# Two linear and two windowed attention layers, forward and backward: score halves at the end of a pass, sums tile by tile, one ring of PSUM banks

## The chip, the cores and the metric

The kernel runs on one core of a Trainium2 chip. The metric is the device time of one execution in microseconds (us); less is better. The engines are TensorE (PE; PEld is its weight loads), VectorE (DVE), ScalarE (ACT), GpSimd (POOL) and SyncE (SP), which issues most DMAs. Matmul results land in PSUM, eight banks of 512 float32 columns for each of 128 partitions; PE writes them, DVE and ACT read them.

## The reference

Four layers over x of 2048 x 640 (bfloat16), 32 heads of 20 columns, then the gradients of the input and of the four weights. A is linear attention, B is softmax attention over the last 256 positions. A and B are applied twice with the same weights.

```python
def _A_ref(x, wqkv, wo):
    ...
    phi = lambda t: jnp.where(t > 0, t + 1, jnp.exp(t)) + 1e-6
    pq, pk = phi(q), phi(k)
    kv = jnp.einsum("bhsd,bhse->bhde", pk, v)
    z = jnp.einsum("bhsd->bhd", pk)
    num = jnp.einsum("bhqd,bhde->bhqe", pq, kv)
    den = jnp.einsum("bhqd,bhd->bhq", pq, z)[..., None] + 1e-6
    o = num / den
    ...
def _B_ref(x, wqkv, wo):
    ...
    scores = jnp.einsum("bhqd,bhkd->bhqk", q, k) * (Dh ** -0.5)
    mask = (idx[:, None] - idx[None, :] >= 0) & (idx[:, None] - idx[None, :] < W)
    scores = jnp.where(mask[None, None], scores, -1e9)
    p = _softmax(scores, axis=-1)
    o = jnp.einsum("bhqk,bhkd->bhqd", p, v)
    ...
x = x + _A_ref(_layernorm(x, axis=-1), A_wqkv, A_wo)
x = x + _B_ref(_layernorm(x, axis=-1), B_wqkv, B_wo)
x = x + _A_ref(_layernorm(x, axis=-1), A_wqkv, A_wo)
x = x + _B_ref(_layernorm(x, axis=-1), B_wqkv, B_wo)
```

kv and z of an A layer are sums over all 2048 positions: no position of the layer's output can be had before the last position has been added.

## The kernel before

Positions are cut into 16 tiles of 128 (tt, or b in the B layers), and columns into five blocks of 128 (m). The forward function has a first part for layer 0, which computes keys and values of all tiles (`a_first`, `a_qkv`), and two passes, `ab_pass(0)` and `ab_pass(2)`. A pass takes each tile through the rest of an A layer (`a_num`: products with the sums; `out_proj` with Wo_A) and the following B layer (`b_qkv`, `attn`, `out_proj` with Wo_B). The first pass also runs `a_first` of layer 2, some two tiles behind; the second pass also prepares gradients of the output (`dO`, with its multiplication on POOL at L830).

The order of the work is made by a planner (`Sched`). Each piece of work names its engine, an estimated duration, and the things that it reads and writes; pieces are listed by a due time in tiles. The planner then runs a list schedule over the engines: the earliest ready piece comes first, and on PE a piece may overtake at most twelve others. What results is a fixed order for each engine. On the chip each engine works through its order and waits where data isn't there.

The sums. In layer 0 `kv_tile` (L609, L611) adds one tile at a time to two PSUM banks, as soon as keys and values of the tile are there. For layer 2 `a_kv` does it after all tiles, one column block at a time over 16 tiles (L571), and z after them (L583), in the banks of the general ring. The sums are multiplied by a block mask into `mbd` (L590), z is copied (L595) and spread over the heads (L597); `a_num` uses both at L647 and L480, and DVE's first use of its result is `rt` (L651).

B attention. A tile has eight groups (g) of four heads. `scores` computes a group's scores for three key tiles (nkt is 3 from the third tile on) in twelve matmuls of 128 columns (L734); head hh uses rows 32 hh to 32 hh + 31 of PE's array and bank hh of the four-bank tile `s_ps`. ACT takes the exponential of all four banks at once into an `e_sb` buffer, of which there are three (L739). POOL masks the diagonal in two instructions of two heads each (L743) and the far edge of the second two heads (L751), DVE that of the first two (L748). `values` multiplies with v (L768), two heads at a time (p_ is 0 or 1), into `pv_ps`, one bank for sixteen heads; DVE reads it at L775 and L776.

The eight PSUM banks of the passes are three of the general ring `mm_ps` (projections, transposes, a_num), four of `s_ps` and one of `pv_ps`. In a ring with `free=True` a piece takes whichever bank is free first, and the last free bank is kept for the piece that is next in the list.

`dO_start` clears two slabs on DVE (L792) in memory that held keys and values of tiles 13 and 14.

Of the kernel before, what the change touches and what calls it, by code (L numbers as in the profile page):

```python
# [11 lines left out]
ALU = mybir.AluOpType  # L12
# [4 lines left out]
P = 128  # L17
# [212 lines left out]
class Kern:  # L230
# [130 lines left out]
    def forward(self):  # L361
# [7 lines left out]
        with ExitStack() as st:  # L369
# [194 lines left out]
            def a_kv(l):  # L564
                def band_sum(m, lo, hi):
                    w_ = hi - lo
                    ps = R["mm"].buf()
                    for t0 in range(0, TT, 4):
                        def f(t0=t0):
                            for tt in range(t0, t0 + 4):  # L570
                                nc.tensor.matmul(ps.t[:, 0:w_], lhsT=pk(tt, m * P, (m + 1) * P), rhs=vv(tt, lo, hi),  # L571
                                                 start=(tt == 0), stop=(tt == TT - 1))
                        op("PE", pe([w_] * 4), f, [k for tt in range(t0, t0 + 4) for k in
                                                   (("pk", tt, 2), ("pk", tt, 3), ("vv", tt, 4), ("vv", tt, 5))], [ps])
                    masked(m, ps, 0)

                for m in range(DT):
                    band_sum(m, *self.band[m])
                zp = R["mm"].buf()
                for m in range(DT):  # L580
                    def f(m=m):
                        for tt in range(TT):
                            nc.tensor.matmul(zp.t[:, m:m + 1], lhsT=pk(tt, m * P, (m + 1) * P),  # L583
                                             rhs=self.ones_bf[:, 0:1], start=(tt == 0), stop=(tt == TT - 1))
                    op("PE", pe([1] * TT), f, [("pk", tt, i) for tt in range(TT) for i in (2, 3)], [zp])
                store_mbd(l, zp, 0)

            def masked(m, ps, off):
                lo, hi = self.band[m]
                op("DVE", vp(hi - lo), lambda: nc.vector.tensor_mul(  # L590
                    mbd[:, m, lo:hi], ps.t[:, off:off + hi - lo], self.bmask[:, m, 0:hi - lo]), [ps, "masks", "zeros"],
                   [("mbd", m)])

            def store_mbd(l, zp, off):
                op("DVE", vp(DT), lambda: nc.vector.tensor_copy(zcol, zp.t[:, off:off + DT]), [zp], ["zcol"])  # L595
# [7 lines left out]
            def kv_tile(tt, sums):  # L603

                def f():
                    for m, (lo, hi) in enumerate(self.band):
                        i, off = at_[m]
                        lhsT = pk(tt, m * P, (m + 1) * P)
                        nc.tensor.matmul(sums[i].t[:, off:off + hi - lo], lhsT=lhsT, rhs=vv(tt, lo, hi),  # L609
                                         start=(tt == 0 and m == 0), stop=(tt == TT - 1), skip_group_check=True)  # L610
                        nc.tensor.matmul(sums[1].t[:, zoff + m:zoff + m + 1], lhsT=lhsT, rhs=self.ones_bf[:, 0:1],  # L611
                                         start=(tt == 0 and m == 0), stop=(tt == TT - 1), skip_group_check=True)
                op("PE", pe([hi - lo for lo, hi in self.band] + [1] * DT), f,
                   [("pk", tt, 2), ("pk", tt, 3), ("vv", tt, 4), ("vv", tt, 5)], sums)
# [100 lines left out]
            def attn(l, b, qT, kTs, vts, oT, out):  # L715
# [10 lines left out]
                def scores(g):  # L726
                    def f():
                        s = R["s"].buf()

                        def mm_s():  # L730
                            for j in range(nkt):
                                for hh in range(4):
                                    r = slice(HPAD * hh, HPAD * (hh + 1))
                                    nc.tensor.matmul(s.t[:, hh, j * P:(j + 1) * P], lhsT=kTs[j].t[r, g, :],  # L734
                                                     rhs=qT.t[r, g, :], start=True, stop=True,
                                                     tile_position=(HPAD * hh, 0))
                        op("PE", 210 + 55 * nkt, mm_s, [qT] + kTs, [s])
                        e = es[g] = R["e"].buf()
                        op("ACT", av(4 * nkt * P), lambda: nc.scalar.activation(  # L739
                            e.t[:, :, 0:nkt, :], s.t[:, :, 0:nkt * P].rearrange("p h (i q) -> p h i q", q=P),  # L740
                            ACT.Exp, scale=self.c_att), [s], [(e, p_, j) for p_ in (0, 1) for j in range(nkt)])
# [14 lines left out]
                def values(g, p_):  # L756
                    def f():
                        e = es[g]
                        q = 4 * g // 16
                        if q not in pvs:  # L760
                            pvs[q] = R["pv"].buf()
                        pv = pvs[q]

                        def mm_pv():
                            for hh in (2 * p_, 2 * p_ + 1):
                                h = 4 * g + hh
                                for j in range(nkt):
                                    nc.tensor.matmul(pv.t[:, h % 16, :], lhsT=e.t[:, hh, j, :],  # L768
# [3 lines left out]
                        if g % 4 == 3 and p_ == 1:  # L772
                            h0 = 16 * q
                            li = lambda: lv.t[:, i_, h0:h0 + 16]
                            op("DVE", 200, lambda: nc.vector.reciprocal(li(), pv.t[:, :, DH]), [pv], [(lv, i_, q)])  # L775
                            op("DVE", vp(16 * DH), lambda: nc.vector.tensor_tensor(  # L776
                                out=o.t[:, h0 * DH:(h0 + 16) * DH].rearrange("p (h d) -> p h d", d=DH),
                                in0=pv.t[:, :, 0:DH], in1=li().unsqueeze(2).to_broadcast([P, 16, DH]), op=ALU.mult),
# [146 lines left out]
            def ab_pass(l, last):  # L925
# [81 lines left out]
                else:  # L1007
                    a_first(items, l + 2, 2.09, -0.2)
                run(items)
# [779 lines left out]
```

## Time and profile before

| | us |
|---|---|
| median of 3 runs (lowest, highest) | 2114.66 (2114.49, 2114.9) |
| profiled execution | 2109.33 |
| its span, first to last instruction | 2107.4 |
| layer 0's keys, values and sums | up to about 77 |
| first pass, last exponential's end | 387.26 |
| first use of layer 2's sums on DVE | 409.11 |
| second pass, last exponential's end | 700.59 |
| first scores of the backward phase on PE | 706.27 |

A line of the timeline gives start, duration, engine, line of the program, operation, what it writes and reads, and how many instructions were merged; in brackets the idle time before it and who ended it. A row of the windows gives, for a stretch, each engine's busy time and number of instructions, the clock that PE was granted, the DMA engines' share and their rate. A row of the waits gives who waited for whom, and the sum, the number of times and the longest. Matmuls are pipelined: the duration of one is its latency, and what it costs is the distance from start to start.

### The profile page before, as it was taken

To read this page: it belongs to the slowest core of one execution; us is meant where nothing else is said; L and a number is where in the kernel's file an instruction comes from. 1 tells how busy PE (TensorE), PEld (TensorE's weight loads), DVE (VectorE), ACT (ScalarE), POOL (GpSimd) and SP (SyncE) were. 2 spreads that over 40 slices of the span, in tenths; PEclk is the share of its full clock that TensorE was granted. 3 is DMA by queue.
4 is the path that set the end of the run, shared out by engine and by line. 5 is a ranking of instruction groups with operands and counts; after the bars stand their busy time and mean duration, and the time that the engine had idled before them with its cause. 6 is when DMAs were issued, how large, how long until landed. Compare 5 with 4: busy or idle time off the path is not lost. (4 is left out here: it accounts for less than half of the span.)

```text
span 2107.4 us, 68065 instructions
## 1 busy us (share of the span) xinstructions
PE 1982.7 (94%) x28001; PEld 1362.9 (65%) x28001; DVE 1437.3 (68%) x2978; ACT 1169.3 (55%) x1946; POOL 840.8 (40%) x1851
## 2 busy tenths in 40 slices
PE   7889999799898899999999999999999999999999
PEld 5656555566555577777665677656777776666764
DVE  8767776567776799999143369606999994444641
ACT  5367888358777688887222223215888872211330
POOL 1044555236666666665022213203666652221210
PEclk9999999899999899999999999998999999999999
DMA  8689877379998699997999999738889879899973
GB/s 309 196 189 216 180 180 184 109 175 195 211 202 191 129 151 165 159 156 122 190 200 191 256 209 207 181 97 159 139 144 144 147 122 183 190 204 241 212 172 90
DMA packets 926568, 373.72 MB, mean 177 GB/s; under 512 B 816944, under 2 KB 902960, under 8 KB 926000
## 3 DMA queue, kind: packets, MB, share of 16 engines
q1 hardware_dynamic: 885616, 337.77, 79.3%
q10 hardware_dynamic: 40640, 31.60, 5.2%
q8 instruction: 219, 3.59, 0.7%
q14 instruction: 93, 0.76, 0.1%
HBM read 106.73 MB, written 112.23 MB: 104 GB/s over the span
## 5 line engine op out<-in xcount | busy, mean ns | idle before, releaser
L1606 DVE SCALAR_TENSOR_TENSOR ds_sb<-pair,e_sb 128x768 bf16<-128x768 f32 x480 | 439.4, 952 | 18.8 <-POOL e_sb L1595 6.8
L1591 ACT ACTIVATE e_sb<-pair 128x768 bf16<-128x768 f32 x480 | 379.1, 812 | 96.1 <-PE pair L1571 94.8
L739 ACT ACTIVATE e_sb<-s_ps 128x1536 bf16<-128x1536 f32 (+2 forms) x256 | 350.6, 1370 | 98.7 <-PE s_ps L734 56.6
L743 POOL TENSOR_SCALAR_AFFINE_SELECT e_sb<-e_sb 128x256 bf16<-128x256 bf16 x512 | 213.2, 439 | 378.2 <-ACT e_sb L739 361.0
L1098 PEld LDWEIGHTS <-om 128*128 128x128 bf16 x1920 | 188.3, 98 | 157.0 <-DMA om<-o 2.2
L1098 PE MATMUL mm_ps<-wq,dqT 128*128 128x320 bf16 x1920 | 276.0, 299 | 4.7 <-ACT dqkv L1430 3.7
L1259 POOL TENSOR_TENSOR gw<-w,gcar 128x640 f32<-128x640 f32 x64 | 89.9, 1405 | 456.7 <-ACT w L1256 451.2
L1098 PE MATMUL mm_ps<-dqkv,om 128*128 128x480 bf16 x1280 | 268.9, 367 | 1.4 <-DMA om<-hn 1.4
L1598 POOL TENSOR_SCALAR_AFFINE_SELECT e_sb<-e_sb 128x256 bf16<-128x256 bf16 x448 | 182.1, 406 | 199.9 <-ACT e_sb L1591 199.9
L1595 POOL TENSOR_SCALAR_AFFINE_SELECT e_sb<-e_sb 128x256 bf16<-128x256 bf16 x512 | 206.5, 407 | 78.5 <-ACT e_sb L1591 78.5
L1098 PEld LDWEIGHTS <-dqT 128*128 128x128 bf16 x1920 | 185.9, 98 | 79.0 <-issue 6.6
L1241 ACT ACTIVATE dh<-mm_ps 128x320 f32<-128x320 f32 x128 | 56.0, 437 | 292.0 <-PE mm_ps L1098 234.3
L1624 PE MATMUL dsT_ps<-ident,ds_sb 128*128 128x128 bf16 x2244 | 189.5, 221 | 3.8 <-DVE dsT L1627 1.3
L480 PE MATMUL mm_ps<-Wqkv_B,hnTB 128*128 128x320 bf16 x960 | 180.4, 300 | 10.7 <-DMA hnTB<-hnB 6.5
L768 PEld LDWEIGHTS <-e_sb 128*128 128x128 bf16 x2880 | 122.2, 97 | 74.7 <-POOL e_sb L751 20.0
L768 PE MATMUL pv_ps<-v_slab,e_sb 128*128 128x32 bf16 x2880 | 145.0, 178 | 19.0 <-DVE oB L776 4.6
L1627 DVE COPY dsT<-dsT_ps 128x768 bf16<-128x768 bf16 x268 | 147.8, 552 | 7.7 <-PE dsT_ps L1624 4.7
L480 PE MATMUL mm_ps<-Wqkv_A,pqT 128*128 128x320 bf16 x780 | 139.2, 302 | 5.8 <-DVE oA L657 2.4
L1571 PE MATMUL pair<-VTg,dOTg 32*128 32x384 bf16 (+2 forms) x896 | 139.9, 318 | 1.0 <-ACT e_sb L1591 0.3
L1624 PEld LDWEIGHTS <-ds_sb 128*128 128x128 bf16 x2244 | 132.4, 98 | 12.1 <-issue 9.3
L1645 PE MATMUL dqvk_ps<-Qsl,ds_sb 128*128 128x32 bf16 x2880 | 134.7, 177 | 3.2 <-ACT dqkv L1627 2.7
L1261 DVE SCALAR_TENSOR_TENSOR gcar<-hn,sm,gw 128x640 bf16<-128x640 bf16 x64 | 80.4, 1256 | 82.0 <-POOL gw L1259 82.0
(178 smaller groups left out, 3556.5 us busy)
## 6 DMA issues: line engine op xcount, KB each, us to landing
qkvp<-qk_slab SPq DMA_DIRECT2D x32, 512.0 KB, 3.1
om<-o SPq DMA_DIRECT2D x20, 512.0 KB, 5.9
hn<-hn SPq DMA_DIRECT2D x64, 160.0 KB, 3.0
om<-hn SPq DMA_DIRECT2D x20, 512.0 KB, 4.9
ee<-e SPq DMA_DIRECT2D x32, 320.0 KB, 3.7
e<-ee SPq DMA_DIRECT2D x52, 160.0 KB, 2.0
qkvp<-v_slab SPq DMA_DIRECT2D x32, 256.0 KB, 2.7
o<-o SPq DMA_DIRECT2D x48, 160.0 KB, 3.4
```

The lines of the kernel that those rows point to most:

```text
L480: nc.tensor.matmul(ps.t[:, w0:w0 + width], lhsT=lhsT(), rhs=rhs(), start=start, stop=stop)
L739: op("ACT", av(4 * nkt * P), lambda: nc.scalar.activation(e.t[:, :, 0:nkt, :], s.t[:, :, 0:nkt * P].rearrange("p h (i q) -> p h i q", q=P) ...
L743: op("POOL", 440, lambda p_=p_: nc.gpsimd.affine_select(out=e.t[:, 2 * p_:2 * p_ + 2, nkt - 1, :], in_=e.t[:, 2 * p_:2 * p_ + 2, nkt - 1, ...
L768: nc.tensor.matmul(pv.t[:, h % 16, :], lhsT=e.t[:, hh, j, :], rhs=vts[j].t[:, h, :], start=(j == 0), stop=(j == nkt - 1))
L1098: nc.tensor.matmul(ps.t[:, w0:w0 + width], lhsT=lhsT(), rhs=rhs(), start=start, stop=stop)
L1571: nc.tensor.matmul(ps[:, i, c0:c0 + len(ks) * P], lhsT=ld[g][lhs][r, q * P:(q + 1) * P], rhs=ld[g][rhs][r, ks[0] * P:(ks[-1] + 1) * P], st ...
L1591: nc.scalar.activation(e, PR[h][:, :, 0:3 * P].rearrange("p i (j q) -> p i j q", q=P), ACT.Exp, scale=self.c_att)
L1595: nc.gpsimd.affine_select(out=e[:, :, j, :], in_=e[:, :, j, :], compare_op=ALU.is_ge, fill=0.0, base=0, pattern=[[0, 2], [-1, P]], channel ...
L1598: nc.gpsimd.affine_select(out=e[:, :, j, :], in_=e[:, :, j, :], compare_op=ALU.is_ge, fill=0.0, base=-1, pattern=[[0, 2], [1, P]], channel ...
L1606: nc.vector.scalar_tensor_tensor(out=DS[n][:, hs], in0=PR[h][:, :, 0:3 * P].rearrange("p i (j q) -> p i j q", q=P), scalar=self.c_att, in1 ...
L1624: nc.tensor.transpose(ps[:, i, j, :], DS[n][:, 2 * p + i, j, :], self.ident)
L1627: (nc.vector.tensor_copy if eng == "DVE" else nc.scalar.copy)(out, in_)
```

## The change

- In the last twelve groups of a pass (b is 14 with g from 4, and b is 15) scores and exponential are made in two halves of two heads, each with its own two banks of `s_ps` as its key. All other groups are as before. Masks and values are unchanged, but a mask now depends on its own half.
- `a_kv` is gone. `kv_tile` is used for layer 2 too, listed in the first pass behind its scores; the sums lie in banks 2 and 3 of `s_ps`, so the first tile waits for the last second-half exponential, and the second pass's scores wait until `store_mbd` has read the sums. All five masked products and z's copy follow the last tile.
- `pv_ps` is gone; `values` takes a bank of `mm_ps`, which now has four.

```diff
-            def a_kv(l):
...
+            def store_mbd(l, sums, keys=()):
+                for m, (lo, hi) in enumerate(self.band):
+                    i, off = at_[m]
+                    op("DVE", vp(hi - lo), lambda m=m, lo=lo, hi=hi, i=i, off=off: nc.vector.tensor_mul(
+                        mbd[:, m, lo:hi], sums[i][:, off:off + hi - lo], self.bmask[:, m, 0:hi - lo]),
+                       ["sums", "masks", "zeros"] + list(keys), [("mbd", m)])
+                op("DVE", vp(DT), lambda: nc.vector.tensor_copy(zcol, sums[1][:, zoff:zoff + DT]), ["sums"] + list(keys), ["zcol"])
...
-            def kv_tile(tt, sums):
+            def kv_tile(tt, sums, keys=None):
...
-                   [("pk", tt, 2), ("pk", tt, 3), ("vv", tt, 4), ("vv", tt, 5)], sums)
+                   [("pk", tt, 2), ("pk", tt, 3), ("vv", tt, 4), ("vv", tt, 5)], ["sums"] if tt else ["sums"] + (keys or []))
...
                 def scores(g):
                     def f():
-                        s = R["s"].buf()
...
                         e = es[g] = R["e"].buf()
+                        for h0, h1 in ((0, 2), (2, 4)) if 2 * b * G + 2 * g >= (2 * TT - 3) * G else ((0, 4),):
+                            halves = range(h0 // 2, h1 // 2)
+
+                            def mm_s(h0=h0, h1=h1):
+                                for j in range(nkt):
+                                    for hh in range(h0, h1):
+                                        r = slice(HPAD * hh, HPAD * (hh + 1))
+                                        nc.tensor.matmul(s_ps[:, hh, j * P:(j + 1) * P], lhsT=kTs[j].t[r, g, :],
+                                                         rhs=qT.t[r, g, :], start=True, stop=True,
+                                                         tile_position=(HPAD * hh, 0))
+
+                            def exp(h0=h0, h1=h1):
+                                nc.scalar.activation(
+                                    e.t[:, h0:h1, 0:nkt, :],
+                                    s_ps[:, h0:h1, 0:nkt * P].rearrange("p h (i q) -> p h i q", q=P),
+                                    ACT.Exp, scale=self.c_att)
+                            op("PE", 210 + 55 * nkt, mm_s, [qT] + kTs, [("s_ps", p_) for p_ in halves])
+                            op("ACT", av((h1 - h0) * nkt * P), exp, [("s_ps", p_) for p_ in halves],
+                               [(e, p_, j) for p_ in halves for j in range(nkt)])
...
-                            pvs[q] = R["pv"].buf()
+                            pvs[q] = R["mm"].buf()
...
                     a_first(items, l + 2, 2.09, -0.2)
+                    for tt in range(TT):
+                        items.append((max(16.1 + 0.15 * tt, tt + 3.9), len(items), lambda tt=tt: kv_tile(
+                            tt, [s_ps[:, i, :] for i in (2, 3)], [("s_ps", 1)])))
...
-            R["mm"] = banks(pool("mm_ps", **PS), 3, "mm_ps")
-            R["s"] = Ring(1, tiles=[pool("s_ps", **PS).tile([P, 4, 512], F32, name="s_ps")])
-            R["pv"] = ring("pv_ps", 1, [P, 16, 32], F32, **PS)
+            R["mm"] = banks(pool("mm_ps", **PS), 4, "mm_ps")
+            s_ps = pool("s_ps", **PS).tile([P, 4, 512], F32, name="s_ps")
             ab_pass(0, False)
-            a_kv(2)
+            store_mbd(2, [s_ps[:, i, :] for i in (2, 3)], [("s_ps", 1)])
             ab_pass(2, True)
```

More of the change, by code (lines that the diff above doesn't have):

```diff
@@ L562, in a_qkv @@
                 return [chunk(ci) for ci in cis]
-            def a_kv(l):
[L565 to L595, printed above, removed]
+            def store_mbd(l, sums, keys=()):
[5 more added lines that the diff above has]
+                op("DVE", vp(DT), lambda: nc.vector.tensor_copy(zcol, sums[1][:, zoff:zoff + DT]), ["sums"] + list(keys), ["zcol"])
@@ L727, in f @@
                     def f():
-                        s = R["s"].buf()
[L730 to L736, printed above, removed]
@@ L1020, in forward @@
             sums_p = pool1("sums_ps", **PS)
-            sums = [Ring(1, tiles=[sums_p.tile([P, 512], F32, name=f"sums{i}")], name="sums").buf() for i in range(2)]
+            sums = [sums_p.tile([P, 512], F32, name=f"sums{i}") for i in range(2)]
             items = []
@@ L1031, in forward @@
             run(items)
-            for m in range(DT):
-                masked(m, sums[at_[m][0]], at_[m][1])
-            store_mbd(0, sums[1], zoff)
+            store_mbd(0, sums)
             S.emit()
```

15 lines of the change are left out of this document (6 added, 9 removed).

## The prediction

> **What bounds the kernel now.** I read the page first, for the shares of the engines.
>
> ```profile
> span 2107.4 us, 68065 instructions
> PE 1982.7 (94%) x28001; PEld 1362.9 (65%) x28001; DVE 1437.3 (68%) x2978; ACT 1169.3 (55%) x1946; POOL 840.8 (40%) x1851
> ```
>
> TensorE (PE) is busy 94% of the span, so the time is PE work plus PE's holes. The changed code runs only in the forward phase, up to about 707 us. Next I read the busy time by stretch, with the stretches cut at the places that the change touches: the last twelve score groups of the first pass, what follows them up to the first use of the second linear layer's sums, and the same for the second pass.
>
> ```profile
> core 0: us, PE busy (x) PEld busy (x) DVE busy (x) ACT busy (x) POOL busy (x), PEclk, DMA share, GB/s
> 362.47:387.26 24.79, 20.48 (x346) 13.63 (x344) 13.29 (x38) 19.32 (x20) 14.21 (x36) 0.86 0.30 97
> 387.26:409.11 21.85, 17.85 (x258) 14.30 (x257) 13.03 (x41) 3.90 (x11) 1.17 (x3) 0.99 0.29 101
> 676.98:700.59 23.61, 18.17 (x323) 12.21 (x321) 12.23 (x30) 17.40 (x12) 15.24 (x37) 0.86 0.50 129
> ```
>
> In neither score tail (first and third row) is any engine full, and the clock is down to 0.86: something goes in series there. The timeline of ScalarE (ACT) and PE in the second pass's tail shows what.
>
> ```profile
> 676.98 1.45 ACT L739 ACTIVATE e_sb<-s_ps 128x1536 bf16<-128x1536 f32 x1 [0.19 <-issue]
> 678.92 1.45 ACT L739 ACTIVATE e_sb<-s_ps 128x1536 bf16<-128x1536 f32 x1 [0.50 <-POOL e_sb L743]
> 699.14 1.45 ACT L739 ACTIVATE e_sb<-s_ps 128x1536 bf16<-128x1536 f32 x1 [0.61 <-POOL e_sb L743]
> ...
> 678.48 0.35 PE L734 MATMUL s_ps<-QT,KT 32*128 32x128 bf16 x12 [0.33 <-ACT e_sb L739]
> 678.76 0.58 PE L480 MATMUL mm_ps<-Wo_B,oTB 128*128 128x320 bf16 x3
> ```
>
> It is a ring of two steps. The exponential ends at 678.43 (676.98 + 1.45), PE starts the next group's scores 0.05 later, having waited for it, and 0.44 after that the next exponential starts: 1.45 + 0.05 + 0.44 = 1.94 us a group, 23.61 us for the twelve from 676.98 to 700.59 (699.14 + 1.45). The score buffer is single, so ACT idles 0.50 a group although nothing else asks for it. The row's releaser (POOL) had long been done; it is the scores. Scores keep PE 0.28 us (678.48 to 678.76). The first pass's tail has the same ring, with small ACT jobs in its gaps.
>
> ```profile
> 362.47 1.45 ACT L739 ACTIVATE e_sb<-s_ps 128x1536 bf16<-128x1536 f32 x1 [0.18 <-issue]
> 363.81 0.43 ACT L544 ACTIVATE ee<-mm_ps 128x320 bf16<-128x320 f32 x1
> 385.81 1.45 ACT L739 ACTIVATE e_sb<-s_ps 128x1536 bf16<-128x1536 f32 x1 [0.46 <-POOL e_sb L743]
> ```
>
> Its twelve exponentials take from 362.47 to 387.26. One occupies ACT 1.34 us (362.47 to the next job at 363.81).
>
> **The change part by part.**
>
> *Scores in halves, both tails.* Twenty-four exponentials of 768 columns replace twelve of 1536 in each pass. The backward phase runs that shape; the third row is the other POOL job in the second pass's tail:
>
> ```profile
> 706.70 0.81 ACT L1591 ACTIVATE e_sb<-pair 128x768 bf16<-128x768 f32 x1 [6.11 <-PE pair L1571]
> 707.40 0.81 ACT L1591 ACTIVATE e_sb<-pair 128x768 bf16<-128x768 f32 x1
> ...
> 689.37 1.34 POOL L830 TENSOR_TENSOR kv<-kv 128x640 f32<-128x640 bf16 x1
> ```
>
> 0.81 us each, 0.70 from start to start. Two halves cost ACT 1.40 against 1.34, so 0.06 more a group; in exchange the scores of one half are computed while the other half is in ACT. The ring of one half is 0.81 + 0.05 + at most 0.44 = 1.30, under the 1.40 that ACT needs for both, so ACT can run without a gap. POOL's masks fit under 1.40 too (15.24 busy less the one L830 below, over twelve: 1.16), and the three e buffers give 3 x 1.40 = 4.2 us for exponential, masks and values. Floor of the second pass's tail: 24 x 0.70 = 16.8 against 23.61, so a gain between 0 and 6.8. In the changed program's order PE's other work stands in pieces of 0.15 to 0.85 us between the half scores, and five times in the two tails both halves stand back to back; each piece above some 0.4 us makes a half late. I take two thirds, **-4.4 us**. Floor of the first pass's tail: 16.8 plus ACT's other jobs there, 19.32 - 12 x 1.34 = 3.2, together 20.0 against 24.79: between 0 and -4.8, and these jobs no longer fall into gaps; I take **-3.5 us**. The masks of the last half begin when its first half has been masked already, one mask of 0.4 us less behind the last exponential: **-0.4 us** at the end of the second pass (in the first it is in the next part).
>
> The price on PE of a half's six matmuls is not in the trace. Twelve over four row groups start 0.28/12 = 23 ns apart. With two row groups the same group comes round after two instead of four, so six cost between 0.14 (same spacing) and 0.28 us (the same 93 ns for one row group). At the worst a tail gets 12 x 0.28 = 3.4 us more PE work, in stretches whose PE has holes of 4.3 and 5.4 us (24.79 - 20.48 and 23.61 - 18.17) and half-clock work besides: nothing on the path.
>
> ```profile
> L734 PE MATMUL s_ps<-QT,KT 32*128 32x128 bf16 x2880 | 87.1, 220 | 9.8 <-ACT e_sb L739 9.0
> ```
>
> The Trainium skill (TensorE: Matmul & The Clock Gate, Part 3: Packing small matmuls, The mechanism) says that a weight load overlaps a running matmul only when the row group differs. What that would do here is the second rival below; the row speaks against it in part, since at 23 ns a row group is loaded again 93 ns after a matmul that takes 220.
>
> *Sums of the second linear layer tile by tile.* Now they are a burst in front of the second pass; the first layer does them tile by tile already.
>
> ```profile
> 400.68 0.65 PE L571 MATMUL mm_ps<-gcar 128*128 128x140 bf16 x8
> 406.95 0.42 PE L647 MATMUL mm_ps<-mbd,pqT 128*128 128x320 bf16 x3
> ...
> 41.94 0.22 PE L609 MATMUL sums<-gcar 128*128 128x140 bf16 x1
> 42.38 2.20 PE L480 MATMUL mm_ps<-Wqkv_A,pqT 128*128 128x320 bf16 x15
> ```
>
> The burst is 6.27 us (400.68 to 406.95) after 0.75 us done earlier; by tiles it is 16 x 0.44 (41.94 to 42.38) = 7.04 us. So no PE work is saved: what can be gained is PE's idle time in this stretch, 21.85 - 17.85 = 4.0 us, which the tiles may fill. Against this stands what hid behind the burst. The five masked products and the column of z run on VectorE (DVE) now while the burst goes on; afterwards they all stand behind the last tile. The first layer shows that form:
>
> ```profile
> 74.56 0.49 DVE L538 CAST kv<-mm_ps 128x320 bf16<-128x320 f32 x1 [0.56 <-PE mm_ps L480]
> 75.44 1.17 DVE L590 TENSOR_TENSOR mbd<-sums,bmask 128x140 bf16<-128x140 f32 x5 [0.39 <-PE sums L609]
> 78.52 0.19 DVE L651 TENSOR_SCALAR rt<-mm_ps 128x32 f32<-128x32 f32 x1 [1.03 <-PE mm_ps L647]
> ...
> 400.88 0.49 DVE L538 CAST kv<-mm_ps 128x320 bf16<-128x320 f32 x1 [0.93 <-PE mm_ps L480]
> 408.16 1.03 DVE L792 MEMSET kv<- 128x512 uint32 x2
> 409.11 0.13 DVE L651 TENSOR_SCALAR rt<-mm_ps 128x32 f32<-128x32 f32 x1
> ```
>
> From the last tile's copy to the first use of the sums it is 3.96 us there (74.56 to 78.52) and 8.23 here (400.88 to 409.11): **4.3 us** less behind the copy. The two memsets, now in this chain, come before the masks in the changed order and lie beside the last tile's matmuls. But the copy itself comes later, because the tiles stand on PE among the links of the last tile's own chain: after the transposes of its attention output PE issues three tiles and two blocks of five matmuls before both blocks of the output projection are through.
>
> ```profile
> 390.77 0.44 PE L495 MATMUL mm_ps<-ident,oB 128*128 128x128 bf16 x5
> 391.05 0.84 PE L480 MATMUL mm_ps<-Wqkv_A,pqT 128*128 128x320 bf16 x5
> 391.80 1.53 PE L480 MATMUL mm_ps<-Wo_B,oTB 128*128 128x320 bf16 x10
> 393.22 1.52 PE L480 MATMUL mm_ps<-Wqkv_A,pqT 128*128 128x320 bf16 x10
> ```
>
> The transposes take 0.28 (390.77 to 391.05) and a 320-column matmul 0.14 (ten from 391.80 to 393.22). So that link grows from 2.45 us (390.77 to 393.22) to 0.28 + 3 x 0.44 + 20 x 0.14 = 4.4 us. Further on, where PE idles for DVE and ACT now, a tile is free. Of the 4.3 I give back 2.7: 2.0 for this link, 0.7 for the rest; **-1.6 us**, between +1 and the -4.0 of the idle time. The sums hold banks 2 and 3 of the scores until the masks have read them; the next scores need the second pass's first projections, which need the sums themselves, so this wait costs nothing.
>
> *One ring of four banks.* The values' bank joins the three of the others, so the second half of a tile's heads no longer waits until DVE has read the first.
>
> ```profile
> PE mm_ps L480 <- DMA hnTB<-hnB: 6.5, 5, 2.3
> PE pv_ps L768 <- DVE oB L776: 4.6, 10, 0.8
> PE pv_ps L768 <- DVE kv L776: 4.1, 5, 0.9
> PE mm_ps L480 <- DVE pp L548: 3.3, 13, 0.8
> PE mm_ps L480 <- DVE qk_slab L699: 2.3, 7, 0.3
> PE mm_ps L480 <- DVE oA L657: 2.3, 7, 0.4
> ```
>
> In 100 to 660 us PE waits 8.7 us for that read (4.6 + 4.1) and 7.9 us for a bank of the other three. The first can go; the second grows while two value banks are held and two are left. Bounds -8.7 and +7.9 (the bank waits doubled); PE is nearly full here and takes a freed wait up with the next one: **-2 us**. SP has the same transfers in a slightly other order, at zero; what hides them is PE's queue of other work, and if that fails the price is one wait for hnTB, up to 2.3 us.
>
> **Sum.** -4.4 - 3.5 - 0.4 - 1.6 - 2 = -11.9 us. The profiled execution took 2109.3 (span 2107.4), 5.3 under the median of the runs; the difference is applied to the median: 2114.66 - 11.9 = 2102.8 us. The backward phase is untouched and moves as a block.
>
> **The rivals.**
>
> 1. *Both tails reach the floor and the value waits all go:* -6.8 - 4.8 - 0.4 - 1.6 - 5 = -18.6, 2096 us. For it: the ring of a half has 0.1 us to spare, and a denser PE would keep the clock up (0.86 now). Against: the large pieces between the halves.
> 2. *Halves without gain.* If two row groups make every second matmul wait for the one before it in its row group, a half takes 3 x 0.22 = 0.66 us and 24 of them 15.8 us. The first pass's tail has some 45 matmuls of 320 columns besides, 6.3 us, and 144 of the values', six in 0.16 (rows below), 3.8: 25.9 us of PE work, more than the 24.79 of now. Or PE's order makes each second half late, and the gap that was filled is back. Both leave -1.6 - 2 = -3.6, 2111 us, within the noise: the change would not do what it says.
>
> ```profile
> 679.46 0.32 PE L768 MATMUL pv_ps<-v_slab,e_sb 128*128 128x32 bf16 x6
> 679.62 0.43 PE L480 MATMUL mm_ps<-Wo_B,oTB 128*128 128x320 bf16 x2
> ```
>
> 3. *The junction gives nothing:* the tiles among the last tile's links delay the copy by the whole 4.3 us: -10.3, 2104.4 us.
> 4. *Slower: the ring runs dry.* A tile opens two value banks, 64 openings in all; at each, until DVE has read the old one, only two banks serve the projections, and a projection waits for one read (0.49 us, as L538 above). At 0.3 us an opening it is 64 x 0.3 = 19 us against gains of 9.9: 2124 us. It decides from 0.15 us an opening. For it: PE already waits 7.9 us with three banks. Against: 27 waits in 32 tiles is less than one a tile, so the third bank is rarely what is missed.
>
> **How the numbers follow.** Forecast 0.53, first rival 0.17, second 0.12, third 0.12, fourth 0.06. A measurement of this kernel tells 0.2%, 4.2 us, from no change. Forecast, first and third rival are faster, and a sixth of the second: 0.84; the rest of the second is the same: 0.10; slower 0.06. The range from 2095 (first rival with a bit more) to 2112 (second) leaves out the slower case and the far ends. The likeliest time is 2102.8.
>
> **What would show it.** In the profile after: half exponentials of 0.81 with starts 0.70 to 0.85 apart, tails of about 21.3 and 19.2 us; from the last exponential of the first pass to the first rt some 20.3 instead of 21.85; first backward scores near 694; no wait of values for the read of oB, and bank waits not above 8 us. It is wrong if halves start 0.95 or more apart, if six scores take 0.5 us, or if waits for qk_slab, pp and oA add up to 15 us.

## The result, and the profile after

| | before | after |
|---|---|---|
| median (lowest, highest), runs | 2114.57 (2112.77, 2114.90), 4 | 2133.61 (2128.85, 2136.64), 4 |
| ratio | | 1.0079, 95% interval 1.0063 to 1.0095 |
| profiled execution (span) | 2109.33 (2107.4) | 2133.86 (2132.1) |

The change made the kernel slower by 0.8%, 19 us from median to median. The forecast was 2102.8, and the range ended at 2112. From the page after:

```profile
span 2132.1 us, 68133 instructions
PE 2007.8 (94%) x28001; PEld 1373.2 (64%) x28001; DVE 1435.8 (67%) x2978; ACT 1173.8 (55%) x1970; POOL 843.6 (40%) x1851
```

The same 28001 matmuls, 24 more instructions on ACT (1970 for 1946), and 24.7 us more span. PE's share is the 94% of before, with 25.1 us more busy time (2007.8 - 1982.7). Such a line says that PE took longer, and not why. The busy time by stretch, cut at the same places as in the prediction (first tail, junction, second tail; columns as there: length, busy time and count of PE, PEld, DVE, ACT and POOL, granted clock, DMA share, GB/s), says where.

```profile
360.73:395.01 34.28, 28.41 (x327) 15.49 (x326) 12.02 (x34) 20.59 (x31) 15.04 (x37) 0.61 0.22 70
395.01:415.80 20.79, 19.36 (x275) 15.88 (x274) 14.00 (x43) 4.25 (x12) 0.80 (x2) 0.98 0.43 124
689.11:721.19 32.08, 25.42 (x323) 14.94 (x322) 10.50 (x29) 19.00 (x24) 16.56 (x38) 0.61 0.34 92
```

The two tails were to fall from 24.79 and 23.61 us to 21.3 and 19.2. They rose to 34.28 and 32.08, together 18.0 us more, while ACT's busy time in them is only 1.3 and 1.6 us up: ACT waits more. The junction fell from 21.85 to 20.79. The other differences of these two profiles, 5.4 us from the junction to the second tail and 4.1 behind it, are not found again in a second pair of profiles (before_same_chip and change_same_chip in the table below). In the timeline of ACT and then of PE at the start of the second tail of after one sees the wait.

```profile
691.10 0.81 ACT L716 ACTIVATE e_sb<-s_ps 128x768 bf16<-128x768 f32 x1 [0.48 <-issue]
692.34 0.81 ACT L716 ACTIVATE e_sb<-s_ps 128x768 bf16<-128x768 f32 x1 [0.43 <-PE s_ps L711]
693.63 0.81 ACT L716 ACTIVATE e_sb<-s_ps 128x768 bf16<-128x768 f32 x1 [0.48 <-PE s_ps L711]
...
691.96 0.34 PE L711 MATMUL s_ps<-QT,KT 32*128 32x128 bf16 x6 [0.43 <-ACT e_sb L716]
692.24 0.58 PE L480 MATMUL mm_ps<-Wo_B,oTB 128*128 128x320 bf16 x3
693.20 0.34 PE L711 MATMUL s_ps<-QT,KT 32*128 32x128 bf16 x6 [0.39 <-ACT e_sb L716]
```

The exponential of one half ends at 691.91 (691.10 + 0.81). The scores of the *other* half start 0.05 later, at 691.96, after PE has stood idle 0.43 for it. They keep PE 0.28 (691.96 to 692.24), and the next exponential starts at 692.34. So the ring is the old one, exponential then scores then exponential, passed once for each half: 1.24 us (691.10 to 692.34) instead of the 0.70 to 0.85 that was predicted. Two rounds are 2.48 us a group, where one round of the whole group was 1.94. In these rows there is no time in which the scores of one half are made while the other half is in ACT. Over both tails most halves start 1.24 to 1.54 apart. In five places of the first tail and four of the second PE makes the scores of both halves back to back, and their exponentials start 0.71 apart; where longer pieces of other PE work stand in between, it is up to 2.73.

The instructions of the changed program say the same: the semaphore value that PE awaits before the scores of a half is that of the exponential of the other half, the last instruction of ACT on the tile `s_ps`. The planner has a key for each half; but both halves lie in one PSUM tile, and the waits are put in by tile.

A second effect follows. In the same tail some 15 us later the clock is at half, and PE's step of the ring is longer (ACT, PE, and the row of the windows):

```profile
706.46 0.81 ACT L716 ACTIVATE e_sb<-s_ps 128x768 bf16<-128x768 f32 x1 [0.59 <-PE s_ps L711]
708.00 0.81 ACT L716 ACTIVATE e_sb<-s_ps 128x768 bf16<-128x768 f32 x1 [0.73 <-PE s_ps L711]
...
704.38 0.50 PE L711 MATMUL s_ps<-QT,KT 32*128 32x128 bf16 x6 [0.25 <-ACT e_sb L716]
704.82 0.50 PE L750 MATMUL mm_ps<-v_slab,e_sb 128*128 128x32 bf16 x12
...
704.00:709.00 5.00, 4.08 (x57) 2.31 (x59) 0.95 (x3) 2.76 (x4) 2.17 (x6) 0.50 0.01 2
```

Six scores take 0.44 (704.38 to 704.82) instead of 0.28, and starts are 1.54 apart (706.46 to 708.00). The 4.08 of 5 us that PE looks busy are 57 matmuls at half speed.

For the ring of four banks, the waits of PE in 100 to 660 us of after:

```profile
PE s_ps L711 <- ACT e_sb L716: 8.3, 21, 0.9
PE mm_ps L750 <- POOL e_sb L732: 4.5, 14, 0.5
PE mm_ps L750 <- DVE e_sb L729: 3.8, 10, 0.6
...
PE mm_ps L480 <- DVE oB L758: 3.0, 5, 1.2
PE mm_ps L480 <- DVE kv L758: 1.9, 5, 0.4
PE mm_ps L480 <- DVE oA L632: 1.4, 4, 0.4
PE mm_ps L480 <- DVE pp L548: 1.0, 5, 0.3
```

No value matmul waits for the read of the old value bank (8.7 us before), and the waits for a bank of the ring are 7.3 us in all, under the 7.9 of before: that part did what was said of it. But the value matmuls (L750) now wait 8.3 us for the masks of `e_sb`. Before, these waits were 4.7 us:

```profile
PE pv_ps L768 <- DVE e_sb L748: 2.5, 5, 0.9
PE pv_ps L768 <- POOL e_sb L751: 2.2, 6, 0.4
```

So part of the freed wait is taken up by the next one, as the prediction said of a PE that is nearly full.

### The profile page after: what moved, and what is told of

Read it like the earlier page. It is cut to its first block, busy times and chain, and to the rows that moved or that the text cites. A ratio compares the mean times of both kernels' runs of the same rounds, so it can differ in the third digit from the quotient of the medians.

```text
span 2132.1 us, 68133 instructions
## 1 busy us (share of the span) xinstructions
PE 2007.8 (94%) x28001; PEld 1373.2 (64%) x28001; DVE 1435.8 (67%) x2978; ACT 1173.8 (55%) x1970; POOL 843.6 (40%) x1851
## 5 line engine op out<-in xcount | busy, mean ns | idle before, releaser
L716 ACT ACTIVATE e_sb<-s_ps 128x1536 bf16<-128x1536 f32 (+3 forms) x280 | 353.9, 1267 | 114.0 <-PE s_ps L711 80.7
L1080 PE MATMUL mm_ps<-dqkv,om 128*128 128x480 bf16 x1280 | 267.9, 366 | 0.8 <-DMA om<-hn 0.8
L750 PEld LDWEIGHTS <-e_sb 128*128 128x128 bf16 x2880 | 127.1, 97 | 68.6 <-POOL e_sb L732 21.5
L750 PE MATMUL mm_ps<-v_slab,e_sb 128*128 128x32 bf16 x2880 | 152.3, 179 | 11.7 <-POOL e_sb L732 5.1
```

Of the source, the lines that this page charges most:

```text
L716: nc.scalar.activation(e.t[:, h0:h1, 0:nkt, :], s_ps[:, h0:h1, 0:nkt * P].rearrange("p h (i q) -> p h i q", q=P), ACT.Exp, scale=self.c_att)
L750: nc.tensor.matmul(pv_h()[:, h % 16, :], lhsT=e.t[:, hh, j, :], rhs=vts[j].t[:, h, :], start=(j == 0), stop=(j == nkt - 1))
L1080: nc.tensor.matmul(ps.t[:, w0:w0 + width], lhsT=lhsT(), rhs=rhs(), start=start, stop=stop)
```

## The experiments

The runs were made on more than one chip; the kernel before had medians of 2124.34, 2116.73 and 2115.99 us beside the three groups of runs, so times are compared by the ratio to before within a group. Times in us in the first expectations are on the scale of the first result, where before took 2114.57; a ratio times that number is what to hold against them. The table gives, from the timeline of each run's profile, the start of the first tail (the first exponential of the last twelve groups), its length, the time from its end to the first rt of the second pass, from there to the second tail, the second tail's length, and what remains of the span after it, nearly all of it the backward phase that no kernel changes. That last column differs by 14 us without cause in the kernels, which says how far one profile can be trusted for single microseconds.

| run | first tail starts | first tail | to rt | to second tail | second tail | rest |
|---|---|---|---|---|---|---|
| before | 362.47 | 24.79 | 21.85 | 267.87 | 23.61 | 1406.8 |
| before_same_chip | 366.32 | 24.88 | 21.89 | 271.06 | 24.23 | 1409.9 |
| the change | 360.73 | 34.28 | 20.79 | 273.31 | 32.08 | 1410.9 |
| change_same_chip | 362.83 | 33.12 | 21.66 | 270.60 | 32.93 | 1410.5 |
| two_tiles | 358.10 | 20.48 | 20.12 | 270.65 | 19.08 | 1413.5 |
| whole_groups | 361.86 | 24.66 | 19.41 | 269.92 | 24.52 | 1416.2 |
| halves_only | 366.10 | 31.78 | 23.94 | 269.86 | 34.22 | 1413.9 |
| ring_only | 362.34 | 24.45 | 21.39 | 273.76 | 24.70 | 1420.7 |
| sums_only | 364.37 | 25.66 | 19.52 | 274.02 | 23.61 | 1416.3 |

The theory to be tested, called W: the scores of a half wait for the other half's exponential because of the shared tile, and this is the loss. Against it: the halves are dear in themselves, or the loss comes from the ring of four or the sums.

**Two score tiles.** The halves get a tile of two banks each, in place of one tile of four; outside the tails, and for whole groups, the four banks are one tile as before. The physical banks and the order of PE's work are the same.

```diff
+                            part = h0 // 2 if h1 - h0 == 2 else None
...
+                                s_ps = s_of(part)
+                                o = h0
...
-                                        nc.tensor.matmul(s_ps[:, hh, j * P:(j + 1) * P], lhsT=kTs[j].t[r, g, :],
+                                        nc.tensor.matmul(s_ps[:, hh - o, j * P:(j + 1) * P], lhsT=kTs[j].t[r, g, :],
...
-                                    s_ps[:, h0:h1, 0:nkt * P].rearrange("p h (i q) -> p h i q", q=P),
+                                    s_ps[:, 0:h1 - h0, 0:nkt * P].rearrange("p h (i q) -> p h i q", q=P),
...
-            s_ps = pool("s_ps", **PS).tile([P, 4, 512], F32, name="s_ps")
+            s_now, s_stack = {}, st.enter_context(ExitStack())
+
+            def s_of(half=None):
+                mode = "full" if half is None else "half"
+                if mode not in s_now:
+                    s_now.clear()
+                    s_stack.close()
+                    n = 1 if half is None else 2
+                    s_now[mode] = [s_stack.enter_context(tc.tile_pool(
+                        name=f"fw_s{mode}{i}_{len(s_names)}", bufs=1, reuse_waits="tile", **PS)).tile(
+                            [P, 4 // n, 512], F32, name=f"s_{mode}{i}") for i in range(n)]
+                    s_names.append(mode)
+                return s_now[mode][half or 0]
+            s_names = []
...
```

> The change as it stands, in the same order of instructions, but the score banks are two PSUM tiles of two banks each (one for each half) while the halves run, and one tile of four banks elsewhere. Theory W (the scores of one half wait for the exponential of the other half, because both halves lie in one PSUM tile): half exponentials start 0.81 to 0.90 us apart instead of 1.24 to 1.54, the two tails fall from 34.3 and 32.1 us to 20.5 to 22.5 and 19.5 to 21.5, the granted clock in them does not stay at 0.5, and the time is 2103 to 2112 us. Rival R1 (halves are bad in themselves: 24 more instructions on ScalarE, or six matmuls on two row groups, each as dear as twelve on four): the halves still start 1.2 us or more apart, tails 30 us or more, time 2128 to 2137. Rival R2 (the loss sits in the ring of four banks or in the second linear layer's sums): tails unchanged in weight, time above 2125.

Measured: 2105.29 us, ratio 0.991 (0.989 to 0.9931). In the instructions the scores of a half now await the exponential of their own half. The windows of the tails and the junction, and the timeline of ACT and then PE in the second tail:

```profile
358.10:378.58 20.48, 19.66 (x337) 12.19 (x337) 11.67 (x34) 19.73 (x31) 15.16 (x37) 1.00 0.38 119
378.58:398.70 20.12, 18.68 (x270) 15.41 (x266) 13.86 (x42) 4.28 (x13) 0.80 (x2) 1.00 0.44 128
669.35:688.43 19.08, 18.82 (x328) 11.62 (x327) 10.81 (x30) 18.12 (x24) 16.24 (x38) 1.00 0.65 164
```

```profile
676.02 10.58 ACT L720 ACTIVATE e_sb<-s_half 128x768 bf16<-128x768 f32 x14 [0.22 <-PE s_half L714]
694.49 0.81 ACT L1597 ACTIVATE e_sb<-pair 128x768 bf16<-128x768 f32 x1 [6.06 <-PE pair L1577]
...
676.96 0.34 PE L714 MATMUL s_half<-QT,KT 32*128 32x128 bf16 x6
677.23 0.51 PE L754 MATMUL mm_ps<-v_slab,e_sb 128*128 128x32 bf16 x6
677.67 0.34 PE L714 MATMUL s_half<-QT,KT 32*128 32x128 bf16 x6
677.95 0.69 PE L495 MATMUL mm_ps<-ident,kv 128*128 128x128 bf16 x5
```

Fourteen half exponentials run in 10.58 us, with starts 0.76 apart on average and no gap above 0.10, and PE makes scores at 676.96 and 677.67 in the midst of them, without a wait. The tails are 20.48 and 19.08 us, the clock in them is 1.00. PE is busy 18.82 of 19.08: it is the bound now, as in the body of the pass. W's forecast is met or passed: the halves start 0.86 and 0.79 apart on average over the two tails (0.81 to 0.90 was expected), both tails are just under the low end of their ranges, and the ratio gives 2095.5 us on the scale of the first result, under the 2103 to 2112 that was expected. The prediction's own signs hold closely too (tails of 21.3 and 19.2, junction 20.3, first backward scores near 694, measured 693.98). Nothing but the tiles was changed, so the loss is the wait. The Trainium skill (PSUM — Partial Sum Buffer, PSUM bank collisions raise a hardware error) says that two engines run clean on different banks and collide only on the same one; the run agrees, with PE writing two banks at 676.96 while ACT reads the other two. The chip never asked for the wait that the shared tile brought.

**Whole groups.** The change without halves: ring of four and sums tile by tile kept.

```diff
-                        for h0, h1 in ((0, 2), (2, 4)) if 2 * b * G + 2 * g >= (2 * TT - 3) * G else ((0, 4),):
+                        for h0, h1 in ((0, 4),):
```

> The change without the halves: whole groups to the end of each pass, the sums tile by tile in score banks and the ring of four banks kept. Theory W: the tails are those of before (24 to 25 and 23 to 24 us), and the time is 2133.6 less 18 for the tails and less 0 to 3 for the clock after them, 2112 to 2116 us, equal to or just under before. Rival R1 says the same. Rival R2 (ring or sums cost the time): 2125 or more.

Measured: 2119.38, ratio 0.9974 (0.9958 to 0.9991), tails 24.66 and 24.52. Ring and sums together are a gain of some 5.5 us (1.9 to 8.9), and the halves in one tile cost all that and the loss besides: 1.0079 against 0.9974 is 22 us. The ratio is 2109.1 us on the scale of the first result, some 3 us better than expected. Against two_tiles, in the same group of runs, it shows what halves are worth when they do overlap: 14.1 us of median time (2119.38 - 2105.29), of which the two tails give 9.6 us in the profiles; the other 4.5 us are not located.

**Ring alone, sums alone.** The kernel before with one of the two.

```diff
-            R["mm"] = banks(pool("mm_ps", **PS), 3, "mm_ps")
-            R["pv"] = ring("pv_ps", 1, [P, 16, 32], F32, **PS)
+            R["mm"] = banks(pool("mm_ps", **PS), 4, "mm_ps")
...
-                            pvs[q] = R["pv"].buf()
+                            pvs[q] = R["mm"].buf()
```

> The kernel before with the ring of four banks alone (the value matmuls take their bank from it). By the prediction's term: 2 us under before, 2112 to 2113. By the trace of the change, where rt to the second tail took 5.4 us more than before (267.9 to 273.3): if the ring costs that, 2117 to 2120; if the clock after the first tail costs it, 2112 to 2115.

```diff
-            a_kv(2)
+            store_mbd(2, [s_ps[:, i, :] for i in (2, 3)], [("s_ps", 1)])
...
+                    for tt in range(TT):
+                        items.append((max(16.1 + 0.15 * tt, tt + 3.9), len(items), lambda tt=tt: kv_tile(
+                            tt, [s_ps[:, i, :] for i in (2, 3)], [("s_ps", 1)])))
```

> The kernel before with the second layer's sums tile by tile in the score banks alone, whole groups, ring of three and the bank for the values. By the prediction's term: last exponential to the first row sum of the second pass falls from 21.85 us to about 20.3, time 2112 to 2114. If the sums that now stand among the first pass's work cost TensorE what they save at the junction: 2114 to 2116. If they wait on the score tile and hold TensorE up in the first pass: over 2117.

Measured: ring 0.9981 (0.9963 to 0.9998), sums 0.9983 (0.9971 to 0.9996): gains of 4.0 and 3.6 us, each known only to some 3 us, and neither a loss; on the scale of the first result they are 2110.6 and 2111.0, each some 1 us better than expected. The table points to the ring's place: the first tail starts at 358.1 to 362.8 in the five profiles listed with the ring of four and at 362.5 to 366.3 in the four without. From rt to the second tail there is no such difference (269.9 to 273.8 against 267.9 to 274.0); why the second pass gives nothing stays open. In PE's waits from 100 to 660 us of ring_only the 8.7 us for the old value bank are gone, the waits for a bank of the ring are 8.2 us (7.9 before), and the waits of value matmuls for masks are 10.8 us (4.7 before): 2.3 us less in all. For the sums, junction rows of sums_only on DVE, behind a last exponential that ends at 390.03:

```profile
406.76 1.17 DVE L567 TENSOR_TENSOR mbd<-s_ps,bmask 128x140 bf16<-128x140 f32 x5
409.55 0.19 DVE L626 TENSOR_SCALAR rt<-mm_ps 128x32 f32<-128x32 f32 x1 [0.73 <-PE mm_ps L622]
```

From there to rt it is 19.52 us, against 21.85 and 21.89 in the two profiles of before. Of these 2.3 us, 1.6 to 1.7 are lost again before the second pass's first exponential, which stands 22.70 behind rt here and 21.00 and 21.12 before. What that exponential gains, 0.6 to 0.8 us, is less than the 3.6 us of the times; where the rest comes from is not shown.

**Halves alone.** The kernel before with the halves in its one score tile, and nothing else of the change.

```diff
+                        for h0, h1 in ((0, 2), (2, 4)) if 2 * b * G + 2 * g >= (2 * TT - 3) * G else ((0, 4),):
...
```

> The kernel before with the halves alone, both in the one score tile of four banks; ring of three, a bank for the values and the sums in their old place. Theory W: half exponentials 1.24 us apart at full clock and more at a lower one, tails of 32 to 35 us each, time 16 to 20 us over before (ratio 1.0075 to 1.0095). If the loss needs the ring of four or the sums as well: the tails stay under 28 us and the time within 6 us of before.

Measured: 2140.99, ratio 1.0113 (1.0096 to 1.0129), tails 31.78 and 34.22; a little over the expected 1.0095, with the same 1.24 us from half to half:

```profile
373.17 0.81 ACT L741 ACTIVATE e_sb<-s_ps 128x768 bf16<-128x768 f32 x1 [0.56 <-PE s_ps L736]
374.41 0.81 ACT L741 ACTIVATE e_sb<-s_ps 128x768 bf16<-128x768 f32 x1 [0.43 <-PE s_ps L736]
```

So the loss needs neither the ring nor the sums.

**More halves.** With two tiles, halves in the last 24 groups, and in every group with three key tiles.

```diff
-                        for h0, h1 in ((0, 2), (2, 4)) if 2 * b * G + 2 * g >= (2 * TT - 3) * G else ((0, 4),):
+                        for h0, h1 in ((0, 2), (2, 4)) if 2 * b * G + 2 * g >= (2 * TT - 6) * G else ((0, 4),):
```

> The version with two score tiles, halves in the last 24 groups of a pass instead of the last twelve. In the two-tile run TensorE was busy 7.45 of 9.30 us just ahead of the second tail and 9.07 of 10 and 9.64 of 10 before that: if the score ring holds TensorE up there, the twelve groups more give back most of that slack, some 2 us a pass, so 0 to 4 us under the two-tile version (ratio to before 0.989 to 0.991). If ScalarE's 24 more instructions decide instead: up to 3 us over it.

```diff
-                        for h0, h1 in ((0, 2), (2, 4)) if 2 * b * G + 2 * g >= (2 * TT - 3) * G else ((0, 4),):
+                        for h0, h1 in ((0, 2), (2, 4)) if b > 1 else ((0, 4),):
```

> The version with two score tiles, halves in every group with three key tiles. TensorE is busy 92 to 94 of 100 us in the body of the passes, so at most 6 to 8 per cent of some 550 us could be had if the score ring made all of its idle time; the waits shown there are mostly for other tiles, so 0 to 8 us under the two-tile version if the ring decides, up to 6 over it if ScalarE, at 78 to 81 of 100 us and with 0.06 us more for each group of two halves, takes the transposing and evicting work later.

Measured: halves_24 0.9915 (0.9899 to 0.9931), not to be told from two_tiles; halves_all 0.9966 (0.9953 to 0.9978), 11 us more than halves_24 in the same group of runs (2109.28 against 2098.27), where at most 6 us more than two_tiles had been expected, and for another reason. PE's busy time in 100 to 360 us, first of two_tiles, then of halves_all:

```profile
100.00:360.00 260.00, 240.62 (x3825) 156.35 (x3822) 188.09 (x523) 202.85 (x273) 135.94 (x332) 0.99 0.83 190
```

```profile
100.00:360.00 260.00, 246.48 (x3833) 165.34 (x3832) 177.72 (x525) 210.72 (x375) 140.12 (x335) 0.99 0.84 189
```

For eight more recorded matmuls PE is busy 5.9 us more. Six scores of a half that stands alone occupy it 0.28 us (677.67 to 677.95 above), as long as the twelve of a whole group (678.48 to 678.76 in the profile of before). Two halves back to back take little more, 0.29 us together, as these rows of halves_all show:

```profile
200.97 0.36 PE L714 MATMUL s_half<-QT,KT 32*128 32x128 bf16 x12
201.26 0.31 PE L754 MATMUL mm_ps<-v_slab,e_sb 128*128 128x32 bf16 x6
```

So a group in halves costs PE some 0.27 us more where its halves stand apart, and 0.01 where they don't. Counted in the traces of both passes, halves_24 has 68 halves alone and 14 pairs, halves_all 160 and 144. 46 more groups apart and 130 more pairs make 46 x 0.27 + 130 x 0.01 = 13.7 us, and PE's busy time over the whole profile is 14.1 us more (2004.6 against 1990.5). PE is nearly full in the body, so this can account for the 11 us; that ScalarE's additional instructions add nothing is not shown. In a tail with holes on PE the 0.27 us are hidden, but with two tiles the tails have hardly any holes left (18.82 of 19.08).

**More work for PE.** How much of the longer tails is the clock? The change as it stands, with three matmuls behind each half whose results nobody reads.

```diff
+                            if h1 - h0 == 2:
+                                d = R["mm"].buf()
+
+                                def warm(d=d):
+                                    for k in range(3):
+                                        nc.tensor.matmul(d.t[:, 0:CW], lhsT=self.ident, rhs=wsb["Wo_B"][:, k, 0:CW],
+                                                         start=True, stop=True)
+                                op("PE", pe([CW] * 3), warm, ["Wo_B"], [d])
```

> The change as it stands (halves in one score tile), with three more matmuls of 128x320 behind each half in the tails, whose sums nobody reads: 24 x 3 x 0.14 = 10 us of added TensorE work in each tail. It asks how much of the longer tails is the clock. Theory W with a part for the clock: the half exponentials keep their 1.24 us (the added work fits into the 0.81 us in which TensorE waits for ScalarE, or some of it stands before the next scores and makes 1.3 to 1.45), the granted clock in the tails rises from 0.5 to above 0.9, and the tails come to 30 to 33 us instead of 34.3 and 32.1 in spite of the added work. If the clock has no part in it: the tails get longer by what of the 10 us does not fit, 36 us or more. If the clock stays at 0.5 all the same, the run tells nothing of its share and the tails pass 36 us.

> The change as it stands, beside the run above. Ratio to before 1.0063 to 1.0095 as before, half exponentials 1.24 us apart where the clock is full, tails 32 to 35 us, clock 0.5 in most of them.

Measured: 1.0065 (1.0046 to 1.0083) with the work, 1.0059 (1.0039 to 1.0078) for the change beside it, a little under the expected 1.0063: the same, though 144 matmuls were added (60 of each 72 run within the tail, the rest just ahead of it), 20 us at the 0.14 of full clock. The tails, first with the added work, then the change:

```profile
361.63:398.78 37.15, 31.76 (x377) 19.89 (x376) 11.75 (x33) 21.66 (x31) 15.34 (x37) 0.86 0.20 65
690.38:723.07 32.69, 26.53 (x359) 16.96 (x358) 10.47 (x27) 19.43 (x25) 16.58 (x37) 0.95 0.32 88
```

```profile
362.83:395.95 33.12, 26.84 (x327) 14.71 (x326) 11.99 (x34) 20.59 (x31) 15.17 (x37) 0.68 0.23 73
688.21:721.14 32.93, 26.42 (x323) 15.21 (x322) 10.49 (x29) 19.01 (x24) 16.55 (x38) 0.56 0.33 90
```

In the second tail the clock rose from 0.56 to 0.95, and the time stayed in spite of 60 x 0.14 = 8.4 us more work. In the first the clock rose to 0.86, and the tail grew by 4 us: the range of 30 to 33 that was given for both holds for one. The starts of exponentials in the second tail show both effects, first in the change, then with the added work:

```profile
705.01 0.81 ACT L716 ACTIVATE e_sb<-s_ps 128x768 bf16<-128x768 f32 x1 [0.73 <-PE s_ps L711]
706.42 0.81 ACT L716 ACTIVATE e_sb<-s_ps 128x768 bf16<-128x768 f32 x1 [0.59 <-PE s_ps L711]
707.96 0.81 ACT L716 ACTIVATE e_sb<-s_ps 128x768 bf16<-128x768 f32 x1 [0.73 <-PE s_ps L711]
```

```profile
714.41 0.81 ACT L716 ACTIVATE e_sb<-s_ps 128x768 bf16<-128x768 f32 x1 [0.43 <-PE s_ps L711]
715.79 0.81 ACT L716 ACTIVATE e_sb<-s_ps 128x768 bf16<-128x768 f32 x1 [0.57 <-PE s_ps L711]
717.03 0.81 ACT L716 ACTIVATE e_sb<-s_ps 128x768 bf16<-128x768 f32 x1 [0.43 <-PE s_ps L711]
```

In the change, at half clock, starts are 1.41 and 1.54 apart here; with the added work and the clock up they are 1.38 and 1.24. Against this, six starts of that tail are 1.81 to 2.34 apart, where in the change only two were as far apart: added matmuls stand ahead of scores there. So the clock is a part, about 0.16 us a half, and an estimate from these rows for twenty halves at half clock is 3 us of the second tail. The larger part is the ring: with the clock nearly full the tail is still some 8.5 us over that of before, and 24 rounds of 1.24 us would be 29.8 us.

**Before on another chip**, for its profile (in the table).

> The kernel before, for a profile on the chip that the other runs used. Tails of 24 to 25 and 23 to 25 us, last exponential to first row sum 21.4 to 22, first row sum to second tail 268 to 275; if the ring of four gives the prediction's 2 us, its first row sum to the second tail is 1 us or more longer here than in the runs with the ring of four.

One time, 2120.31. Its tails and junction are those of the first profile. Its way from rt to the second tail, 271.06, is no longer than in the runs with the ring of four, against the condition set for the prediction's 2 us.

## Why the prediction was wrong

- *The step that failed* is the sentence "in exchange the scores of one half are computed while the other half is in ACT", under scores in halves, and the sum behind it. The ring of a half was worked out rightly, 0.81 + 0.05 + at most 0.44 = 1.30, and 1.24 was measured. What was taken for granted is that there are two such rings, side by side. With one PSUM tile there is one, and nearly every half takes a round of its own. The prediction's terms of -4.4 and -3.5 became +8.5 and +9.5 in the profiles. The -0.4 behind the last exponential didn't come either: from its end to the first backward scores it is 5.68 us before, 6.70 in the change, and 5.55 with two tiles. The planner's keys for each half were read as the waits of the program; the tile, four banks in one, is named in the quoted diff and was not asked about.
- *The sign was right under its own condition.* "It is wrong if halves start 0.95 or more apart": most start 1.24 to 1.54 apart. With two tiles they start 0.79 and 0.86 apart on average, and the tails of 20.48 and 19.08 us are a little under those forecast, 21.3 and 19.2. That version gains 19 us (15 to 23), more than the sum of 11.9, and where the excess sits is only in part known; its second tail ends 12.2 us earlier than in the first profile of before and 20.0 earlier than in the second.
- *The clock* was used as a gain only (the first rival's denser PE). It works both ways: with PE waiting more, the granted clock in the tails fell from 0.86 to 0.61, and six scores took up to 0.44 us instead of 0.28.
- *The second rival* named late halves, but priced them at no change, because it let the old gap come back once a group. It comes back twice a group. Its other half, two row groups at 0.66 us, did not occur: six scores took 0.28, the upper of the prediction's two bounds. The 23 ns between starts, from which the bounds were worked out, is an average and not the spacing: in the traces four row groups start within 13 ns of each other (678.479 to 678.492 in before), and a row group starts its next matmul 55 to 67 ns after its last, with four row groups (678.479, 678.534, 678.589) as with two (677.675, 677.740, 677.796 in two_tiles). That this costs "nothing on the path" rested on holes on PE that are gone with two tiles.
- *The sums* were right up to rt: 20.3 us was forecast, and 19.4 to 20.1 was measured in whole_groups, sums_only and two_tiles (20.79 and 21.66 in the change itself, whose clock was lower in the tail). Beyond rt the prediction did not look, and there most or all of it is lost: the second pass's first exponential stands 22.70 to 23.33 behind rt in these three, and 21.00 and 21.12 before. *The ring* was right in sign, -2 against a measured -4.0 (-7.9 to -0.4), and PE's waits are 2.3 us less in ring_only, though only the first pass shows it. *The fourth rival*, the ring running dry, was the case for slower, and it was the wrong one: bank waits are 7.3 us.

## What to carry to other kernels

When a buffer is cut so that two engines may work on it at once, look at the waits in the program that is built and not at the dependences of one's own planner: two halves in one PSUM tile were one buffer here, and splitting that buffer's tile, with the banks left where they are, turned a loss of 0.8% into a gain of 0.9%. Before cutting a step of a serial ring in two, work out the ring for the case that the halves do not overlap: it is then passed twice, and every fixed latency in it is paid twice. A cut that costs TensorE time (six matmuls on two row groups for the price of twelve on four) belongs where TensorE has holes, unless the halves stand back to back.

## What the hardware showed that was not expected

- In the second tail of the change the granted clock lay at 0.50 from 696.2 us to the tail's end at 721.19, though PE looked busy 4.08 of 5.00 us (704 to 709): busy time at half clock is no sign of load. The Trainium skill (TensorE: Matmul & The Clock Gate, Part 1: The HAM clock gate) says that the array's clock is halved while its recent activity is low; the runs agree: some 8 us of added matmuls in a tail of 32.93 us brought the clock from 0.56 to 0.95, and the tail was no longer (32.69).
- Six matmuls of 32 rows by 128 columns on two row groups occupy PE as long as twelve on four (0.28 us), and two such sixes on different row groups, back to back, take 0.29 us.
